# First two batches staged in the activation buffer of the feed-forward part, angle tables reduced on GpSimd, weights in gated chunks, second DFT product written densely

## The chip, the cores and the metric

One NeuronCore of a Trainium2 chip runs the whole program. The metric is the device time of one execution in microseconds (us); the times given are medians of timed runs. Engines are named as the profile names them: PE (matrix multiplication), ACT (scalar engine), DVE (vector engine), POOL (GpSimd), SP (the engine that issues most DMAs).

## The reference, cut to what matters

```python
q_n = q / (np.linalg.norm(q, axis=-1, keepdims=True) + 1e-06)      # q, k, v: (8, 12, 448, 64) f32
k_n = k / (np.linalg.norm(k, axis=-1, keepdims=True) + 1e-06)
scores = np.matmul(q_n, k_n.transpose(0, 1, 3, 2)) / tau           # tau = 0.1
attn = softmax(scores)
x = np.matmul(attn, v).transpose(0, 2, 1, 3).reshape(8, 448, 768)
mixed = np.real(np.fft.fft(np.fft.fft(x, axis=1), axis=2))
u = x + mixed
un = (u - mean(u)) / np.sqrt(var(u) + 1e-06)
out = u + np.maximum(un @ w_ch1, 0.0) @ w_ch2                      # w_ch1: (768, 3072), w_ch2: (3072, 768)
```

Every one of the eight batches goes through attention, a two-dimensional DFT, a layer norm and a feed-forward part. The weights are the same for all batches.

## The kernel before

All work is written as operations of a small planner (`Plan`): each has an engine (or two to choose from), an estimated duration, a priority and the names that it reads and writes. `schedule` simulates the engines with these estimates and fixes one order for each engine; `emit` writes the orders out with semaphore waits. At run time each engine takes its instructions strictly in that order, so one that has to wait holds up everything planned behind it.

Four stages are planned for each batch `b`:

- **Normalisation** (`attn`, first half). Seven tiles of 128 rows by 768 f32 are loaded (three of q, three of k, and one `t` with the last 64 rows of both), each as runs of 256 bytes, by SP into one of four staging slots `STG`. ACT squares a tile into `SQT` (L460), DVE sums it by head (L462), ACT takes Ln and Exp (L467, L470), DVE adds epsilon, takes the reciprocal (L472, L474) and scales the tile into a bf16 buffer `QH` (L480), and SP transposes it by DMA into `QT` or `KT` (L492). Four more loads bring v; POOL casts it into `VB` and `VZ`. POOL also copies one column of `QT` (`qdup`, L498), for which the score products wait.
- **Attention** for six pairs of heads: score products (L541 to L555), Exp on ACT (L532), products with v (L569, L572), and the division on DVE (L584, L586) into `X`. DVE then forms sums and differences `AC` (L594, L597).
- **DFT** (`fft`): DVE forms `F` from `AC` (L608), PE multiplies by the table over the sequence, `CSs` (24 matmuls, L622), ACT brings the result to SBUF (L633), PE multiplies by the table over the features, `CSd` (48 matmuls of 193 or 192 columns, L654), DVE adds `X` and writes `U` (L664, L666), and the layer norm writes `UN`, which SP transposes by DMA into `unT` (L704). There is one `UN` buffer, so each of three or four normalised tiles waits for the transposition ahead of it.
- **Feed-forward** (`ffn`): 24 groups `h` of six matmuls (L729) with Relu into `hT`, and then the products with `w_ch2` (L750), added to `U` (L759) and stored by SP or, through index lists, by POOL (L773). Batches with even `b` have three tiles of 128 rows, odd ones four.

Attention and DFT of a batch have the higher priority, the matmuls of the feed-forward part the lowest: they fill what is left of PE.

In L654 the output of a matmul goes to every second f32 word of a PSUM bank: `eo` is 0 for the even and 1 for the odd features, so that DVE can read the features in their natural order.

```python
lw = self.Tt[:, o0:o0 + 128]
m0, m1 = (0, 193) if eo == 0 else (193, 385)
...
r = pe.matmul(PS[:, bk + sg, eo:NL:2], lw, mv, start=(s == 0 and dj == 0),
```

The tables are made at the start: DVE forms the angles and reduces them by full turns (L370 to L384), and ACT takes the sines (L389 to L392); `hT`, which is not used yet, holds the temporary values. L393 then loads the table of functions that holds both Ln and Exp. The weights are cast to bf16 on the way by eight DMAs of 2.36 MB of f32 each, which POOL issues once all loads of batch 0 are issued (L405, L410).

## Time and profile before

| | us |
|---|---|
| median of 3 timed runs | 756.86 (756.28 to 757.26) |
| profiled execution, its own time | 761.87 |
| its span, first to last instruction | 760.1 |
| PE busy in the span | 642.2 |
| first matmul of the feed-forward part (L729) starts | 155.36 |

The profiled execution is 5.01 us longer than the median and 1.77 us longer than its span. Busy times of PE are modelled ends of pipelined matmuls; how fast a sequence of matmuls goes is read from the distance between starts.

### The profile page before, as it was taken

The page shows a single profiled execution, that of the slowest core. Times are in us where ns is not written, and L with a number is a line of the kernel's source. Part 1 is how long each engine was busy: PE and PEld are TensorE (multiplying, and loading weights), DVE is VectorE, ACT ScalarE, POOL GpSimd, SP SyncE. Part 2 cuts the span into 40 slices and gives each one's busy share as a digit, 9 for nine tenths or more (in the row PEclk, how much of TensorE's full clock was granted, in tenths as well). Part 3 has the DMA queues.
Part 4 walks back from the last instruction along what each step waited for, and adds up shares of the span by engine and source line. Part 5 has one row for each costly group of instructions (what it writes and reads, how often), then busy time and mean ns, then how long its engine had stood idle before and what let it go on. Part 6 is the DMA issues. An engine that isn't in the chain of part 4 may idle for free.

```text
span 760.1 us, 12228 instructions
## 1 busy us (share of the span) xinstructions
PE 642.2 (84%) x5088; PEld 392.4 (52%) x5088; DVE 343.7 (45%) x649; ACT 331.8 (44%) x561; POOL 62.7 (8%) x93
## 2 busy tenths in 40 slices
PE   0014146699999999999999999999999999999997
PEld 0002124467556556566655565567655756665454
DVE  8422144776665873865645546462244234000011
ACT  3333233764584784366426643463147320412400
POOL 3022001001002001010000010101010001001001
PEclk9999865999999999999999999999999999999999
DMA  4589999157749278526632474254111002101001
GB/s 83 112 159 199 202 194 199 36 98 165 146 89 189 47 129 165 131 54 146 136 87 44 71 139 104 61 108 63 33 42 22 1 22 63 43 22 42 0 22 63
DMA packets 206967, 70.79 MB, mean 93 GB/s; under 512 B 198464, under 2 KB 204608, under 8 KB 206912
## 3 DMA queue, kind: packets, MB, share of 16 engines
q1 hardware_dynamic: 199040, 52.71, 36.8%
q0 software_dynamic: 7872, 17.30, 9.7%
q8 instruction: 40, 0.66, 0.4%
q14 instruction: 15, 0.12, 0.1%
HBM read 51.90 MB, written 11.01 MB: 83 GB/s over the span
## 4 chain that ended last, share of the span: by engine, by line
PE 70%; DMA 13%; DVE 7%; ACT 5%; issue 3%; SPq 2%; POOL 0%; POOLq 0%; DVEq 0%; ACTq 0%
PE PS L729 27%; PE PS L750 23%; PE PS L654 8%; DMA STG<-in_k_dram 7%; PE PS L572 4%; DMA STG<-in_q_dram 3%; PE PS L541 3%; ACT E L532 2%; PE PS L622 2%; DVE QH L480 2%; DMA QT<-QH 1%; PE PS L545 1%; PE PS L569 1%; ACT SQT L460 1%; DVE SS L462 1%
## 5 line engine op out<-in xcount | busy, mean ns | idle before, releaser
L750 PE MATMUL PS<-W2b,hT 128*128 128x384 bf16 x1344 | 227.3, 326 | 0.0
L532 ACT ACTIVATE E<-PS 128x900 bf16<-128x900 f32 x192 | 150.7, 825 | 63.3 <-PE PS L545 56.2
L750 PEld LDWEIGHTS PS<-W2b,hT 128*128 128x128 bf16 x1344 | 129.1, 98 | 86.9 <-issue 5.0
L738 ACT ACTIVATE hT<-PS 128x384 bf16<-128x384 f32 (+1 forms) x153 | 83.0, 543 | 138.7 <-PE PS L729 138.2
L729 PE MATMUL PS<-unTo,W1b 128*128 128x512 bf16 x576 | 133.2, 380 | 0.5 <-DVE OUTB L759 0.5
L541 PE MATMUL PS<-QT,KT 64*128 64x225 bf16 x288 | 38.9, 277 | 85.5 <-POOL QT L498 52.5
L759 DVE TENSOR_TENSOR OUTB<-PS,U 128x384 f32<-128x384 f32 x56 | 31.1, 555 | 160.4 <-PE PS L750 160.3
L729 PE MATMUL PS<-unTe,W1b 128*128 128x384 bf16 x576 | 98.5, 326 | 1.7 <-DMA unTe<-UN 1.7
L462 DVE TENSOR_REDUCE SS<-SQT 128x12 f32<-128x768 f32 x56 | 52.9, 945 | 75.3 <-ACT SQT L460 75.1
L729 PEld LDWEIGHTS PS<-unTo,W1b 128*128 128x128 bf16 x576 | 54.2, 98 | 61.9 <-issue 3.2
L460 ACT ACTIVATE SQT<-STG 128x768 f32<-128x768 f32 x56 | 47.1, 841 | 87.8 <-DMA STG<-in_q_dram 38.7
L729 PEld LDWEIGHTS PS<-unTe,W1b 128*128 128x128 bf16 x576 | 55.4, 98 | 38.2 <-DMA unTe<-UN 2.0
L541 PEld LDWEIGHTS PS<-QT,KT 64*128 64x128 bf16 x288 | 14.2, 95 | 113.8 <-issue 63.0
L654 PE MATMUL PS<-CSd,AC 128*128 128x193 bf16 (+1 forms) x384 | 66.1, 374 | 3.7 <-ACT AC L633 2.9
L654 PEld LDWEIGHTS PS<-CSd,AC 128*128 128x128 bf16 x384 | 53.5, 140 | 15.5 <-ACT AC L633 3.9
L480 DVE TENSOR_TENSOR QH<-STG,RN 128x768 bf16<-128x768 f32 x56 | 55.0, 997 | 5.8 <-DMA KT<-QH 3.5
L572 PE MATMUL PS<-VB,E 128*128 128x65 bf16 x1152 | 55.6, 199 | 0.0
L569 PE MATMUL PS<-VZ,E 128*128 128x130 bf16 x192 | 44.0, 229 | 11.2 <-ACT E L532 9.1
L572 PEld LDWEIGHTS PS<-VB,E 128*128 128x128 bf16 x1152 | 52.2, 102 | 2.0
L773 POOL DMA_INDIRECT out_dram<-OUTB,IDX x20 | 19.6, 978 | 378.1 <-DVE OUTB L759 223.8
L502 POOL CAST VB<-STG 128x768 bf16<-128x768 f32 x24 | 20.4, 848 | 255.4 <-DMA STG<-in_v_dram 162.7
L666 DVE TENSOR_TENSOR U<-PS,X 128x385 bf16<-128x385 f32 (+3 forms) x40 | 22.4, 560 | 35.4 <-PE PS L654 34.7
(74 smaller groups left out, 444.2 us busy)
## 6 DMA issues: line engine op xcount, KB each, us to landing
STG<-in_q_dram SPq DMA_DIRECT2D x24, 384.0 KB, 5.1
STG<-in_k_dram SPq DMA_DIRECT2D x24, 384.0 KB, 5.5
STG<-in_v_dram SPq DMA_DIRECT2D x24, 384.0 KB, 5.3
W1b<-in_moe_w_ch_dram POOLq DMA_DIRECT2D x4, 1152.0 KB, 18.9
W2b<-in_moe_w_ch_dram POOLq DMA_DIRECT2D x4, 1152.0 KB, 43.3
out_dram<-OUTB SPq DMA_DIRECT2D x8, 384.0 KB, 2.3
STG<-in_q_dram SPq DMA_DIRECT2D x8, 192.0 KB, 3.4
STG<-in_k_dram SPq DMA_DIRECT2D x8, 192.0 KB, 4.5
```

The source lines that it names most:

```text
L460: P.add("act", lambda a, s=s: a.activation(self.SQT[:], self.STG[:, s, :], ACTF.Square), t_act(DM), pr, f"sq{i}_{b}", reads=[f"STG{s}"], w ...
L462: P.add("dve", lambda v, i=i: v.tensor_reduce(SS[:, i, :], v3(self.SQT[:]), AX.X, AluOp.add), t_dve(DM), pr, f"ss{i}_{b}", reads=["SQT"], ...
L480: P.add("dve", lambda v, i=i, s=s, r=r: v.tensor_tensor(v3(self.QH[:, r, :]), v3(self.STG[:, s, :]), RN[:, i, :].unsqueeze(2).to_broadcast ...
L532: return a.activation(o, self.PS[:, bk:bk + nc_, 0:SQ2], ACTF.Exp, scale=1.0 / self.tau)
L541: pe.matmul(self.PS[:, bk + h, 0:NK], self.KT[r, j, kt * 128:(kt + 1) * 128], self.QT[r, j, 0:NK], start=True, stop=True)
L569: pe.matmul(o, st(6), self.VZ[:, j, :], start=True, stop=False, skip_group_check=True)
L572: r = pe.matmul(o[:, 65 * h:65 * h + 65], st(2 * kt + h), self.VB[:, kt, 2 * j + h, :], start=False, stop=(h == 1 and kt == 2), skip_group ...
L654: r = pe.matmul(PS[:, bk + sg, eo:NL:2], lw, mv, start=(s == 0 and dj == 0), stop=(s == 1 and dj == 2))
L729: r = pe.matmul(self.PS[:, bk, 0:N], self.W1b[:, j, ft * 128:(ft + 1) * 128], unT[:, j, 0:N], start=(j == 0), stop=(j == NJ - 1))
L738: return e.activation(self.hT[:, ft, 0:N], self.PS[:, bk, 0:N], ACTF.Relu)
L750: r = pe.matmul(self.PS[:, bk, 0:384], self.hT[:, ft, 128 * i:128 * i + 128], self.W2b[:, ft, 384 * c:384 * c + 384], start=(ft == 0), sto ...
L759: return v.tensor_tensor(self.OUTB[:, ob, cs], self.PS[:, self.bank(tile), 0:384], self.U[:, ut, cs], AluOp.add)
```

## The change

- **Staging.** The q, k and `t` tiles of batches 0 and 1 go to `hT`, seven slots of three `hT` tiles each, instead of to the four slots of `STG`. All loads of batch 0 can so be issued at once; loads of v and of batch 1 are ordered behind chosen transpositions of batch 0 (`gates`), those of batch 2 behind the first store of an output. A Relu that writes an `hT` tile waits until batch 1 no longer needs that slot.
- **Squares.** For batch 0 they go to `E`, `SQT` and `OUTB`, so that they don't wait for each other's buffer. For batch 1 POOL multiplies the tile by itself, and all seven tiles form one group with one Ln, Exp and reciprocal. POOL may also scale tiles of batch 0.
- **Tables.** DVE only multiplies (five instead of ten products); POOL reduces 1605 values per row by full turns; cosines come from the sine with a bias of pi/2 and an added Abs on ACT. The sines, and the loading of the common table of Ln and Exp behind them, are planned after the last Exp of batch 0's normalisation.
- **Weights.** 24 chunks of 0.79 MB of f32 instead of eight of 2.36 MB. Each waits until the one two ahead of it has landed. The first chunk of `W1` waits for the last q/k load of batch 1, the first of `W2` for the last transposition of the normalised tiles of batch 0. The products wait for single chunks.
- **DFT product.** The second product writes 193 or 192 adjacent words; DVE reads even and odd features from the two halves with an access pattern.
- **Normalised tiles.** `UN` gets four buffers, which lie in `F`.
- **Planner.** DMAs get a latency and a service time on two shared queues; it knows orders without a wait.

```diff
+        dma_free = [0.0, 0.0]
...
+            if op.dma is not None:
+                i = 1 if e == "pool" and op.serve > 2 else 0
+                t0 = max(op.end + DMA_LAT, dma_free[i])
+                op.end = t0 + op.serve * (1.6 if dma_free[1 - i] > t0 else 1.0)
+                dma_free[i] = op.end
...
-        self.UN = T("UN", [128, DM])
-        self.unT = [T("unTe", [128, NJ, 384]), T("unTo", [128, NJ, 512])]
+        self.UN = self.F[:].rearrange("p a b c -> p (a b c)").rearrange("p (t c) -> p t c", t=4)
+        self.UNT = T("UNT", [128, NJ * 896])
+        self.unT = [self.UNT[:, 0:NJ * 384].rearrange("p (j c) -> p j c", j=NJ),
+                    self.UNT[:, NJ * 384:].rearrange("p (j c) -> p j c", j=NJ)]
...
+        P.add("pool", lambda g: [g.tensor_scalar(Qt[:, c], Pt[:, c], 1.0 / n, M, AluOp.mult, AluOp.add) for c, n in sect][-1],
+              1.9, -4, "tq", reads=["tp"], writes=["tq"])
+        P.add("pool", lambda g: [g.tensor_scalar(Qt[:, c], Qt[:, c], M, -float(n), AluOp.subtract, AluOp.mult)
+                                 for c, n in sect][-1], 1.9, -4, "tr", reads=["tq"], writes=["tq"])
+        P.add("pool", lambda g: g.tensor_tensor(Qt, Pt, Qt, AluOp.add), t_pool(nt, True), -4, "ts", reads=["tp", "tq"], writes=["tq"])
...
+            a.activation(self.CSs[:, :, 0, :], s2(Pt), ACTF.Sin, bias=h, scale=-w / S)
+            a.activation(self.CSs[:, :, 1, :], s2(Qt), ACTF.Sin, scale=w / S)
+            a.activation(self.CSd[:, :, 0, :], d3(Pt), ACTF.Sin, bias=h, scale=-w / DM)
+            a.activation(self.CSd[:, :, 1, :], d3(Qt), ACTF.Sin, scale=w / DM)
+            r = a.activation(self.CSd[:, :, 2, :], d3(Qt), ACTF.Sin, scale=-w / DM)
...
+    def tables(self):
+        P, sins = self.P, self.sins
+        Pt, Qt = self.temps
+        P.add("act", lambda a: a.activation(Pt, Qt, ACTF.Abs), t_act(3 * NL + 2 * NK), 9.5, "ta", reads=["tq"], writes=["tp"],
+              order=self.sq0)
+        P.add("act", sins, 1.3 + 4.3 + 1.3, 10.5, "sins", reads=["tp", "tq", "cst"], writes=["CSs", "CSd"], order=self.nrm0)
...
+    def weights(self, which, start):
         P = self.P
-        g0 = self.first_loads
-        for c in range(4):
-            P.add("pool", lambda g, s, c=c: g.dma_start(
-                self.W1b[:, :, c * 768:(c + 1) * 768],
-                self.w1.rearrange("(j p) f -> p j f", p=128)[:, :, c * 768:(c + 1) * 768]).then_inc(s, 16),
-                1.0, -3, f"w1_{c}", writes=[f"W1_{c}"], dma=(f"w1_{c}", 16), after=g0, lat=7.0 * (c + 1))
-        for c in range(4):
-            P.add("pool", lambda g, s, c=c: g.dma_start(
-                self.W2b[:, c * 6:(c + 1) * 6, :],
-                self.w2.rearrange("(t p) n -> p t n", p=128)[:, c * 6:(c + 1) * 6, :]).then_inc(s, 16),
-                1.0, -3, f"w2_{c}", writes=[f"W2_{c}"], dma=(f"w2_{c}", 16), after=g0, lat=7.0 * (c + 5))
+        prev = [start, start]
+        w1 = self.w1.rearrange("(j p) f -> p j f", p=128)
+        w2 = self.w2.rearrange("(t p) n -> p t n", p=128)
+        for i in range(12 * which, 12 * which + 12):
+            c = i % 12
+
+            def fn(g, s, i=i, c=c):
+                if i < 12:
+                    return g.dma_start(self.W1b[:, :, c * 256:(c + 1) * 256], w1[:, :, c * 256:(c + 1) * 256]).then_inc(s, 16)
+                return g.dma_start(self.W2b[:, c * 2:(c + 1) * 2, :], w2[:, c * 2:(c + 1) * 2, :]).then_inc(s, 16)
+            nm = f"W{1 + i // 12}_{c}"
+            prev.append(P.add("pool", fn, 1.0, 9, nm, writes=[nm], dma=(nm, 16), after=[prev[-2]], serve=2.1))
...
+            if b < 2 and kind != "v":
+                s = self.h_next % 7
+                self.h_next += 1
+                buf = self.hT[:, 3 * s:3 * s + 3, :].rearrange("p a b -> p (a b)").bitcast(F32)
+                names, key = [f"hT{3 * s + x}" for x in range(3)], f"lh{s}"
+            else:
+                s = self.stg_next % NSTG
+                self.stg_next += 1
+                buf, names, key = self.STG[:, s, :], [f"STG{s}"], f"ld{s}"
+
+            def fn(sy, sem):
+                for dst, src in dmas(buf):
                     sy.dma_start(dst, src).then_inc(sem, 16)
-            nd_ = len(dmas(self.STG[:, s, :]))
-            op = P.add("sp", fn, 0.36 * nd_, pr, f"ld_{nm}{b}", writes=[f"STG{s}"], dma=(f"ld{s}", 16 * nd_), lat=3.5)
+            nd_ = len(dmas(buf))
+            op = P.add("sp", fn, 0.36 * nd_, pr, f"ld_{nm}{b}", writes=names, dma=(key, 16 * nd_),
+                       order=[self.trs[gates[nm]]] if b < 2 and nm in gates else [self.first_st] if b == 2 else [],
+                       serve=0.8 if nm == "v3" else 1.6)
...
-        groups = [(0, 1), (2, 3), (4, 5), (6,)]
+        groups = [(0, 1), (2, 3), (4, 5), (6,)] if b != 1 else [tuple(range(7))]
+        if b == 0:
+            gates = dict(zip(("v0", "v1", "v2", "v3"), (1, 2, 3, 3)))
+        elif b == 1:
+            gates = {"q0": 4, "k0": 5, "q1": 6, "k1": 6, "q2": 6, "k2": 6, "t0": 6}
...
+                if b == 1:
+                    op = P.add("pool", lambda g, sq=sq, buf=buf: g.tensor_tensor(sq, buf, buf, AluOp.mult),
+                               t_pool(DM, True), pr, f"sq{i}_{b}", reads=names, writes=[sqn], margin=mg)
+                else:
+                    op = P.add("act", lambda a, sq=sq, buf=buf: a.activation(sq, buf, ACTF.Square),
+                      t_act(DM), pr, f"sq{i}_{b}", reads=names, writes=[sqn], margin=mg)
...
+                P.add(("dve", "pool") if b == 0 else ("dve",), lambda v, i=i, buf=buf, r=r: v.tensor_tensor(
+                    v3(self.QH[:, r, :]), v3(buf),
                     RN[:, i, :].unsqueeze(2).to_broadcast((128, H, DH)), AluOp.mult),
-                    t_dve(DM), pr, f"sc{i}_{b}", reads=[f"STG{s}", f"RN{par}_{i}"], writes=[f"QH{r}"])
+                    (t_dve(DM), t_pool(DM, True)), pr, f"sc{i}_{b}", reads=names + [f"RN{par}_{i}"], writes=[f"QH{r}"])
...
-                                r = pe.matmul(PS[:, bk + sg, eo:NL:2], lw, mv, start=(s == 0 and dj == 0),
+                                r = pe.matmul(PS[:, bk + sg, m0:m1], lw, mv, start=(s == 0 and dj == 0),
...
+                    src = PS[i0:i0 + n, bk, 0:NL]
+                    src = gp(src, [[-1, 192], [192, 2]], 192) if hi else gp(src, [[1, 192], [193, 2]])
+                    cs = slice(384, 768) if hi else slice(0, 384)
+                    return v.tensor_tensor(U[o0:o0 + n, ut, cs].rearrange("p (i e) -> p i e", e=2), src,
+                                           X[i0:i0 + n, x, cs].rearrange("p (i e) -> p i e", e=2), AluOp.add)
...
-            self.main = P.add("pe", fn, 6 * t_mm(N), PM, f"h{ft}_{b}", reads=un + [f"W1_{ft // 6}"], tiles=(tile,),
+            self.main = P.add("pe", fn, 6 * t_mm(N), PM, f"h{ft}_{b}", reads=un + [f"W1_{ft // 2}"], tiles=(tile,),
...
+                n = len(self.loads)
                 self.attn(b + 1)
+            if b == 0:
+                self.weights(0, self.loads[n + 6])
+                self.weights(1, self.last_tru)
```

The planner's new orders differ almost everywhere; three places of the start follow.

ACT in the normalisation of batch 0, **before**; SQT and E hold squares, SS sums of squares:

```order
L389 ACT_TABLE_LOAD
L389 ACTIVATE CSs<-F 128x900 [waits prog_dve]
L391 ACTIVATE CSd<-hT 128x3x770
L392 ACTIVATE CSd<-hT 128x3x385
L393 ACT_TABLE_LOAD
L467 ACTIVATE SS<-SS,cst 128x24 [waits prog_pool,prog_dve]
L460 ACTIVATE SQT<-STG 128x768 [waits prog_act,d_ld2]
L470 ACTIVATE SS<-SS 128x24 [waits prog_act]
```

The same place **in the changed kernel**, where L500 is the square, L511 Ln, L514 Exp:

```order
L500 ACTIVATE E<-hT 128x768 [waits d_lh2]
L511 ACT_TABLE_LOAD [waits prog_pool]
L511 ACTIVATE SS<-SS,cst 128x24 [waits prog_dve]
L500 ACTIVATE E<-hT 128x768 [waits d_lh3]
L514 ACT_TABLE_LOAD
L514 ACTIVATE SS<-SS 128x24 [waits prog_act]
L500 ACTIVATE SQT<-hT 128x768 [waits d_lh4]
L511 ACT_TABLE_LOAD
L511 ACTIVATE SS<-SS,cst 128x24 [waits prog_dve]
L514 ACT_TABLE_LOAD
```

The sines and the loading of the common table have moved behind the four groups of batch 0; in each group Ln and Exp now have a table load of their own, eight in all.

POOL at the weights, **before** (L502 and L506 cast v, L498 is the copy `qdup`):

```order
L498 COPY QT<-QT 128x6 [waits prog_dve,d_QT0,prog_pool,d_QT3,prog_act]
L502 CAST VB<-STG 128x12x64 [waits prog_pool,d_ld1]
L405 DMA W1b<-in_moe_w_ch_dram 128x6x768 [waits prog_pool,d_ld2]
L405 DMA W1b<-in_moe_w_ch_dram 128x6x768 x3
L410 DMA W2b<-in_moe_w_ch_dram 128x6x768 x4
L506 CAST VZ<-STG 64x6x64
```

POOL **in the changed kernel**, from the last squares of batch 1 (L497) to the `qdup` of batch 1 (L546); the left-out rows are five more chunks and the casts of v (L550, L554) between them:

```order
L423 DMA W1b<-in_moe_w_ch_dram 128x6x256 [waits prog_pool,d_lh6]
L423 DMA W1b<-in_moe_w_ch_dram 128x6x256
L497 TENSOR_TENSOR OUTB<-hT 128x768 [waits prog_dve,d_lh5]
L497 TENSOR_TENSOR SQT<-hT 128x768 [waits prog_pool,prog_dve]
L423 DMA W1b<-in_moe_w_ch_dram 128x6x256 [waits prog_pool,d_W1_0]
...
L423 DMA W1b<-in_moe_w_ch_dram 128x6x256 [waits d_W1_8]
L423 DMA W1b<-in_moe_w_ch_dram 128x6x256 [waits d_W1_9]
L424 DMA W2b<-in_moe_w_ch_dram 128x2x768 [waits d_unT0_2]
L424 DMA W2b<-in_moe_w_ch_dram 128x2x768
L546 COPY QT<-QT 128x6 [waits prog_act,d_QT3,d_QT0,prog_dve]
```

The weights now stand behind the loads of batch 1 instead of ahead of them, with waits in POOL's order, and `qdup` of batch 1 stands behind all chunks of `W1` and two of `W2`.

DVE ahead of batch 0's DFT, **before** (L594 to L608 make AC and F of batch 0; L462 to L480 normalise batch 1):

```order
L474 RECIPROCAL RN<-SS 128x24 [waits prog_dve]
L480 TENSOR_TENSOR QH<-STG,RN 128x768 [waits d_ld0,prog_dve,d_KT0]
L584 RECIPROCAL RD<-PS 128x8 [waits prog_pe]
L480 TENSOR_TENSOR QH<-STG,RN 128x768 [waits d_ld3,d_QT0]
L586 TENSOR_TENSOR X<-PS,RD 128x4x128 [waits prog_dve]
L462 TENSOR_REDUCE SS<-SQT 128x12 [waits prog_act]
L594 TENSOR_TENSOR AC<-X 128x2x384 [waits prog_dve]
```

and **in the changed kernel** (L504 sums, L518 adds epsilon for all seven tiles of batch 1, L633 to L647 make AC and F, L526 scales):

```order
L504 TENSOR_REDUCE SS<-OUTB 128x12 [waits prog_pool]
L504 TENSOR_REDUCE SS<-SQT 128x12 [waits prog_pool]
L623 RECIPROCAL RD<-PS 128x8 [waits prog_pe]
L625 TENSOR_TENSOR X<-PS,RD 128x4x128 [waits prog_dve]
L518 TENSOR_SCALAR SS<-SS 128x84 [waits prog_act]
L633 TENSOR_TENSOR AC<-X 128x2x384 [waits prog_dve]
L636 TENSOR_TENSOR AC<-X 128x2x384
L520 RECIPROCAL RN<-SS 128x84 [waits prog_dve]
L647 TENSOR_TENSOR F<-AC 128x1536 [waits prog_dve]
```

Before, scalings and loads of batch 1 through the four slots stood ahead of F; now the sums of all seven tiles of batch 1 do, and no scaling.

## Rows read from the trace of the kernel before

**Rows 1.** Two windows: length; busy PE, PEld, DVE, ACT, POOL; clock, DMA share, GB/s.

```profile
0.00:155.36 155.36, 49.24 (x506) 31.62 (x507) 69.45 (x123) 63.98 (x97) 21.95 (x43) 0.88 0.83 146
155.36:747.00 591.64, 585.33 (x4536) 356.42 (x4537) 272.65 (x524) 267.86 (x465) 38.83 (x48) 1.00 0.38 80
```

**Rows 2.** Chain that ended last, first 160 us: start us, us, what.

```profile
46.01 3.89 DMA QT<-QH
...
52.48 0.37 PE PS L541 x2
...
66.25 41.01 DMA STG<-in_k_dram
...
119.66 4.72 PE PS L622 x24
...
125.37 9.98 PE PS L654 x48
...
155.36 1.15 PE PS L729 x6
```

**Rows 3.** Timeline of PE at the end: start us, us, engine, line, operation.

```profile
645.43 23.56 PE L729 MATMUL PS<-unTe,W1b 128*128 128x384 bf16 x144
...
723.31 31.36 PE L750 MATMUL PS<-W2b,hT 128*128 128x384 bf16 x192
```

**Rows 4.** Chain, DFT products at the high clock: start us, us, what.

```profile
169.51 1.58 PE PS L622 x16
...
174.82 7.83 PE PS L654 x48
```

**Rows 5.** Groups on PE from 160 us on: busy us, mean ns, idle before.

```profile
L569 PE MATMUL PS<-VZ,E 128*128 128x130 bf16 x148 | 32.5, 220 | 1.1 <-ACT E L532 1.1
```

**Rows 6.** Window of the first 20 us; columns as in rows 1.

```profile
0.00:20.00 20.00, 0.00 (x0) 0.00 (x0) 15.21 (x22) 8.03 (x7) 7.08 (x23) 1.00 0.44 79
```

**Rows 7.** Timeline of the start, single instructions; columns as in rows 3.

```profile
0.75 0.46 SPq L431 DMA_DIRECT2D STG<-in_q_dram  x1
...
4.63 0.84 ACT L460 ACTIVATE SQT<-STG 128x768 f32<-128x768 f32 x1 [2.60 <-DMA STG<-in_q_dram]
...
20.27 1.28 ACT L393 ACT_TABLE_LOAD   x1
...
21.57 0.32 ACT L467 ACTIVATE SS<-SS,cst 128x24 f32<-128x24 f32 x1
...
32.45 1.27 SPq L492 DMA_TRANSPOSE KT<-QH  x1
...
53.08 3.02 ACT L532 ACTIVATE E<-PS 128x900 bf16<-128x900 f32 x4 [1.13 <-PE PS L545]
...
56.32 2.98 ACT L532 ACTIVATE E<-PS 128x900 bf16<-128x900 f32 x4 [0.22 <-PE PS L545]
```

**Rows 8.** Groups on POOL: busy us, mean ns, idle before.

```profile
L502 POOL CAST VB<-STG 128x768 bf16<-128x768 f32 x24 | 20.4, 848 | 255.4 <-DMA STG<-in_v_dram 162.7 <-PE PS L572 92.5
...
L405 POOL DMA_DIRECT2D W1b<-in_moe_w_ch_dram x4 | 3.6, 907 | 0.7 <-POOL VB L502 0.7
...
L397 POOL TENSOR_SCALAR CSs<-CSs 1x225 bf16<-1x225 bf16 x2 | 1.6, 792 | 11.9 <-ACT CSd L392 11.9
```

**Rows 9.** Timeline of SP, transpositions of batch 0's normalised tiles.

```profile
143.77 8.56 SPq L704 DMA_TRANSPOSE unTe<-UN  x3
```

**Rows 10.** Tile W1b: from issue to landing.

```profile
DMA to landing us min/median/max: 9.8/18.9/28.2
```

**Rows 11.** Tile W2b: from issue to landing.

```profile
DMA to landing us min/median/max: 34.3/43.3/52.3
```

**Rows 12.** Timeline of PE, two successive products with v, each one pair of 7 matmuls.

```profile
144.87 0.23 PE L569 MATMUL PS<-VZ,E 128*128 128x130 bf16 x1
...
145.12 0.22 PE L569 MATMUL PS<-VZ,E 128*128 128x130 bf16 x1
```

**Rows 13.** Costliest groups of the page: weight loads of the second product.

```profile
L654 PEld LDWEIGHTS PS<-CSd,AC 128*128 128x128 bf16 x384 | 53.5, 140 | 15.5 <-ACT AC L633 3.9
```

More of the change, by code (lines that the diff above doesn't have):

```diff
@@ L105, in add @@
         op.acquire = acquire
+        op.order = tuple(order)
         for t in tiles:
@@ L115, in schedule @@
         for op in self.ops:
-            cnt[op] = len(op.deps)
-            for d in op.deps:
+            cnt[op] = len(op.deps.union(op.order))
+            for d in op.deps.union(op.order):
                 nxt.setdefault(d, []).append(op)
@@ L124, in rtime @@
             for d in op.deps:
-                if d.eng == e and d not in op.raw:
+                if d.eng == e and d.dma is None and d not in op.raw:
                     t = max(t, d.start)
                 else:
-                    t = max(t, d.end + SEM_LAT)
-            return t + op.margin
+                    t = max(t, d.end + SEM_LAT + (op.margin if e == "pe" or d.dma is not None else 0.0))
+            return t
         def put(op):
@@ L394, in sins @@
             return r
-        P.add("act", sins, 1.3 + 4.0 + 1.3, 15, "sins", reads=["tp%d" % S, "tp%d" % DM] + wr, writes=["CSs", "CSd"])
+        self.sins, self.temps = sins, (Pt, Qt)
+    def tables(self):
[4 more added lines that the diff above has]
+        P.add("act", sins, 1.3 + 4.3 + 1.3, 10.5, "sins", reads=["tp", "tq", "cst"], writes=["CSs", "CSd"], order=self.nrm0)
@@ L469, in attn @@
                   0.25, pr, f"ln{b}", reads=ssn + ["cst"], writes=ssn)
-            P.add("act", lambda a, a0=a0, a1=a1: a.activation(SS[:, a0:a1, :], SS[:, a0:a1, :], ACTF.Exp, scale=0.5),
-                  0.2, pr, f"nrm{b}", reads=ssn, writes=ssn)
+            op = P.add("act", lambda a, a0=a0, a1=a1: a.activation(SS[:, a0:a1, :], SS[:, a0:a1, :], ACTF.Exp, scale=0.5),
+                       0.2, pr, f"nrm{b}", reads=ssn, writes=ssn)
+            if b == 0:
+                self.nrm0.append(op)
             P.add("dve", lambda v, a0=a0, a1=a1: v.tensor_scalar_add(SS[:, a0:a1, :], SS[:, a0:a1, :], 1e-6),
@@ L532, in fn @@
                     return a.activation(o, self.PS[:, bk:bk + nc_, 0:SQ2], ACTF.Exp, scale=1.0 / self.tau)
-                P.add("act", fn, t_act(nc_ * SQ2), pj, f"ex{j}_{b}", writes=nm, after=(tile.users[0],), tiles=(tile,))
+                P.add("act", fn, t_act(nc_ * SQ2), pj, f"ex{j}_{b}", writes=nm,
+                      after=[tile.users[0]] + (self.sqb if b == 0 and j < 2 else []), tiles=(tile,))
             for kt in range(3):
@@ L753, in ffn @@
                     self.main = P.add("pe", fn, 6 * t_mm(384), PM, f"y{i}{c}{q4}_{b}",
-                                      reads=[f"hT{ft}" for ft in range(6 * q4, 6 * q4 + 6)] + [f"W2_{q4}"],
+                                      reads=[f"hT{ft}" for ft in range(6 * q4, 6 * q4 + 6)] + [f"W2_{3 * q4 + x}" for x in range(3)],
                                       tiles=(tile,), acquire=(tile if q4 == 0 else None), after=[self.main])
```

161 lines of the change are left out of this document (74 added, 87 removed).

## Prediction

> **What bounds the kernel now.** I read the windows first, split where the feed-forward part starts. From 155.36 us on PE is busy for 585.33 of 591.64 us at the full granted clock, so 6.3 us are lost [rows 1]; every other engine has room. Ahead of that point PE is busy for 49.24 of 155.36 us, much of it at a lower clock. So the kernel is a slow start and then a long stretch of matmuls without gaps: only fewer us of matmul or an earlier start of the stretch count.
>
> The chain says why the start is slow. The first score product runs at 52.48 us; then one load of a k tile of batch 1 is on the chain for 41.01 us, from 66.25 on [rows 2]: it shares the DMA engines with the weights, all issued before. DVE, strictly in order, stands at that tile's sum, with the DFT of batch 0 behind it. The DFT follows at 119.66 and the feed-forward part at 155.36 [rows 2].
>
> The work of the long stretch, from starts of matmuls: two batches of the feed-forward part run from 645.43 to 723.31 + 31.36 = 754.67, so 109.2 us, and 437.0 for eight [rows 3]. The first DFT product takes 1.58/16 = 98.8 ns a matmul, 24 of them 2.37 us; the second takes 7.83 us for 48, 163 ns each [rows 4]; together 10.2. From 155.36 to 754.67 are 599.3 us, less 6.3 idle 593.0; less 437.0 and 7 x 10.2 = 71.4, attention has 84.6. The 148 products with VZ are 37 head pairs [rows 5], and about half a pair runs between 155.36 and 160: 2.26 us a pair. After the last matmul the span lasts 760.1 - 754.7 = 5.4 us.
>
> **The denser DFT product.** The first product writes 225 adjacent words in 98.8 ns, the second 193 words at stride two in 163 ns [rows 4]; both change weights for each matmul. No row shows 193 adjacent words. Bounds: 163 ns (the stride is not the cause) and 98.8 x 193/225 = 84.7 ns. I take the lower, from the row of the same kind of matmul: 48 x 84.7 = 4.07 us, 3.76 less for each DFT, 26.3 for the seven in the long stretch. DVE reads as many words as before, in another pattern; unknown between nothing and twice its time, covered by PE's other work except in the first DFT, where it could add 4 us.
>
> The Trainium skill, "TensorE: Matmul & The Clock Gate", section "LDWEIGHTS", speaks against that much: 128 columns of weights would take some 107 ns, and by it the product would stay at 5.1 us, some 7.5 us less gain in all. This trace disagrees: seven matmuls, each with its own weights, start every 145.12 - 144.87 = 0.25 us, 36 ns apart [rows 12].
>
> **The start in the changed kernel**, step by step, up to the first feed-forward matmul (T):
> - Loads. Four loads in the first 20 us keep the DMA engines busy for 0.44 x 20 = 8.8 us, 2.2 us each [rows 6]. The first, issued at 0.75, is squared at 4.63 [rows 7]: 1.7 us beside its 2.2. The third lands at 9.0, the seventh at 17.8.
> - ACT from 9.0 on has no pause: five squares of 0.84, Abs over 1605 values (1.75 at the rate of a square), eight table loads of 1.28 (this is new: before, the common table came first), four Ln and four Exp of at most 0.32 [rows 7]: 18.8, so 27.8. Two more table loads and the sines of 4365 values, 4.8 us by that rate, keep it to 35.
> - The last tile: 1.4 us on DVE, then a transposition of 3.89 [rows 2] ends at 33, hidden under the sines. Before, 2.6 us lay between landing (49.90) and the first score product (52.48); of these 1.1 remain after 35: 36, against 52.48.
> - Attention of batch 0 at ACT's pace, 56.32 - 53.08 = 3.24 us a pair [rows 7]: 19.4, and 1 to 2 for the last product: 57.
> - Batch 1. SP issues v and then batch 1 behind the last transposition (27.8 + 1.4 + 1.27 [rows 7]), from 30.5 on: 9.5 tiles of 2.2 and 1.7, so the last q/k tile lands at 53. POOL then issues two chunks (0.9 each) and does two squares. The trace has no f32 product on POOL: bounds are a cast of 768 values, 0.85, and a tensor-scalar at 0.79 for 225, 2.7 for 768 [rows 8]. A product reads two inputs where the cast reads one, so I take twice the cast, 1.7: 53 + 1.8 + 3.4 = 58.2. A sum, Ln, Exp and epsilon add 1.8, AC and half of F 2: the DFT of batch 0 starts at 62. It is this wait, not attention's end, that comes last.
> - The DFT. Before, first product to second took 125.37 - 119.66 = 5.7, with 4.72/24 = 197 ns a matmul: twice the 98.8 of later, so the lower clock level [rows 2, 4]. PE comes from a pause again, so I take 5.7, and 2 x 4.07 = 8.1 for the second: 75.8.
> - From there to the feed-forward part: 155.36 - 125.37 - 9.98 = 20.0 before [rows 2]. In that, three transpositions through one buffer took 8.56 us to issue [rows 9]; with four buffers three issues of 1.27 follow each other, 3.8: 15.3. T = 91. Against this stands `qdup`, which waits behind POOL's chunks; see the weights.
>
> Bounds of T: 80 (DFT at the high clock, 6.9 less; squares as fast as a cast, 1.7 less; loads at 2.0 us, 2 less) and 104 (squares at 2.7 on seven tiles that then trail the loads, 4; 20.0 instead of 15.3; slow DVE reads, 4).
>
> **The weights.** Between the landings of the first and the last of four DMAs are 52.3 - 34.3 = 18.0 us [rows 11]: 6.0 each, 2.0 for one third. The first of all took 9.8 [rows 10], 3.8 beside its 6.0. With two in flight a chunk costs (0.9 + 3.8 + 2.0)/2 = 3.35 us; the lower bound is 2.0. W1 then lands until 53 + 12 x 3.35 = 93, W2 at 93 + 40 = 133. `qdup` comes at about 93, when PE has other groups `h`. PE needs the last quarter of W2 after T + 23.4 (24 groups) + 13.6 (attention of batch 1) + 6.4 (its DFT) + 3 of the first output tile, and some 8 of waits: 145. So 12 us to spare, and I cost the chunks at nothing; beyond 4 us a chunk the cover is gone. POOL's 16 more issues lie in its idle time.
>
> The Trainium skill, "DMA: Bandwidth & Descriptors", section "Bandwidth", speaks against the small chunks: it asks for 1 MiB or more per DMA, and its fit (2.0 us plus bytes) would give 3.8 us for one of 0.79 MB, nearly the point where the cover ends if nothing overlapped. No row shows a DMA of this size.
>
> **Sum.** From T on: 437.0 + 42 x 2.26 + 7 x 6.44 = 577.0 of matmuls. Waits: 6.3 before; attention of batch 1 now runs inside the first feed-forward part, at ACT's pace and partly at the lower clock, so I take 12 (6 to 20). 91 + 577.0 + 12 + 5.4 = 685.4, 74.7 less than the span of 760.1. The profiled execution itself took 761.87, the median 756.86; the difference taken off the median gives **682 us**. With the bounds of T and of the waits: 665 to 702, and 668 to 700 as this case's own range.
>
> **Rivals.**
> - *Weights late*: chunks cost 4.5 to 6 us, because a chunk's fixed time isn't hidden. W2 lands at 53 + 24 x 5 = 173 for 5 us, 28 after PE needs it: **710**. For it: waits of POOL in its own order, transposes and v loads among the chunks. Against: 9.8 us for a DMA three times as large, under load [rows 10]. The page on DMA names such a cost.
> - *The product stays as it was*, the stride not being the cause: 682 + 26.3 and 1.9 in the first DFT: **710**. For it: no row of adjacent 193. Against: the dense 225 [rows 4].
> - *Weight loads bound the product*: 48 of 140 ns [rows 13] are 6.7 us instead of 4.07, 2.65 x 7 more: **701**. Against: rows 12. The page on TensorE names weight loads as such a cost.
> - *Slower*: the chunk chain starves PE. The gain of 75 is used up when W2 lands at 145 + 75 = 220, that is at (220 - 53)/24 = 7 us a chunk; at 8 it is 245, and **782**. Against: it needs twice the 3.35.
>
> **Chances.** Forecast 0.65, weights late 0.17, product as before 0.07, weight loads 0.06, slower 0.04, and 0.01 for a chunk right at 7 us, which ends within 0.2%, about what a measurement of this kernel can tell from no change. So faster 0.95, same 0.01, slower 0.04. The range 666 to 714 leaves out the slower case, the late half of the late weights and the edge of the forecast, under 2 in 10.
>
> **What would show it.** L693 at 4.1 us for 48 matmuls at the full clock (not 7.8); eight table loads ahead of the sines; first score product at 36; the last square of batch 1 on POOL ahead of the first matmul of the DFT, at 62; first L770 at 91; chunks of weights every 3.4 us, and no wait of PE's L791 for a DMA. The forecast is wrong if L693 keeps 163 ns, if POOL's squares take over 3 us, or if PE waits for W1b, W2b or `qdup` for more than 10 us.

## The result, and the profile after

The changed kernel takes **684.86 us** (median of four runs, 679.65 to 685.53) against 757.06 for the kernel before on the same chip: ratio 0.903, with a 95% interval of 0.899 to 0.908. The forecast was 682, the range 666 to 714. It is near, but partly by luck: the start was 6 us longer than forecast, the waits behind it 10 us shorter, and 5 us were taken off at the end without a reason.

The windows of the changed kernel, split at the first feed-forward matmul, columns as in [rows 1]:

```profile
0.00:97.35 97.35, 27.43 (x324) 18.82 (x325) 55.25 (x88) 51.94 (x69) 48.98 (x61) 0.84 1.10 162
97.35:676.73 579.38, 577.50 (x4764) 350.49 (x4764) 280.02 (x541) 284.05 (x490) 48.40 (x62) 1.00 0.48 94
```

The long stretch starts 58 us earlier than in [rows 1] and has 1.9 us of idle PE where 6.3 were. It ends with the last products:

```profile
645.37 31.36 PE L791 MATMUL PS<-W2b,hT 128*128 128x384 bf16 x192
```

The second DFT product, by the page's costliest groups and by the timeline of batch 1's DFT: 4.01 us from its start to the start of what follows, 83.5 ns a matmul, where [rows 4] had 163. (The 253 ns of the group's row are the length of one record; the records of successive matmuls overlap.) DVE's sums that read the new layout take 550 ns each, no more than before (560).

```profile
L693 PE MATMUL PS<-CSd,AC 128*128 128x193 bf16 (+1 forms) x384 | 35.1, 253 | 1.6 <-ACT AC L672 1.6
...
L706 DVE TENSOR_TENSOR U<-PS,X 128x384 bf16<-128x384 f32 (+3 forms) x80 | 40.6, 550 | 35.1 <-PE PS L693 34.0
```

```profile
141.75 4.18 PE L693 MATMUL PS<-CSd,AC 128*128 128x193 bf16 x48
145.76 1.46 PE L791 MATMUL PS<-W2b,hT 128*128 128x384 bf16 x8
```

The start is shown by a timeline of single instructions. There are table loads between ACT's Ln and Exp, the first score product comes at 34.19 ([rows 2]: 52.48), and then comes the place that the forecast missed. The last sum of squares (L504) is done at 57.9, but ACT stands for 6.65 us at a copy of half of batch 1's v tail (L824), the last 64 rows of v, which have not landed yet, and Ln (L511) is behind it:

```profile
4.67 0.84 ACT L500 ACTIVATE E<-hT 128x768 f32<-128x768 f32 x1 [2.66 <-DMA hT<-in_q_dram]
9.14 1.28 ACT L511 ACT_TABLE_LOAD   x1
...
24.60 1.28 ACT L514 ACT_TABLE_LOAD   x1
25.89 0.21 ACT L514 ACTIVATE SS<-SS 128x12 f32<-128x12 f32 x1
...
34.19 0.37 PE L580 MATMUL PS<-QT,KT 64*128 64x225 bf16 x2 [34.19 <-POOL QT L546]
...
55.42 1.47 POOL L497 TENSOR_TENSOR SQT<-hT 128x768 f32<-128x768 f32 x1
56.92 0.95 DVE L504 TENSOR_REDUCE SS<-SQT 128x12 f32<-128x768 f32 x1 [0.59 <-POOL SQT L497]
...
61.62 0.53 ACT L824 ACTIVATE VZ<-STG 64x384 bf16<-64x384 f32 x1 [6.65 <-DMA STG<-in_v_dram]
62.18 0.36 ACT L511 ACTIVATE SS<-SS,cst 128x84 f32<-128x84 f32 x1
...
66.46 4.70 PE L661 MATMUL PS<-CSs,F 128*128 128x225 bf16 x24 [10.23 <-DVE F L647]
72.18 5.86 PE L693 MATMUL PS<-CSd,AC 128*128 128x193 bf16 x48 [1.01 <-ACT AC L672]
97.35 7.80 PE L770 MATMUL PS<-UNT,W1b 128*128 128x384 bf16 x30 [19.31 <-DMA UNT<-F]
```

From the DFT's end (78.04) to the feed-forward part are 19.3 us. The end of this stretch, on the chain: the last normalised tile is ready at 87.6, but SP (L745) is then still issuing the transposition of the second tile, until 91.42. The last one is issued at 91.47 and lands 5.84 us later. Beside it POOL issues weight chunks until 92.49.

```profile
87.10 0.47 DVE F L741
87.58 0.88 DVE QH L526
88.45 2.96 SPq L745
91.42 0.05 issue
91.47 5.84 DMA UNT<-F
```

SP's timeline has the three tiles (L745) and a transposition of batch 1 between them. The second of the three takes 3.51 us to issue, the first 1.21; they land 8.1, 8.7 and 5.8 us after the start of their issue:

```profile
84.48 1.21 SPq L745 DMA_TRANSPOSE UNT<-F  x1
85.88 1.97 SPq L538 DMA_TRANSPOSE QT<-QH  x1
87.91 4.98 SPq L745 DMA_TRANSPOSE UNT<-F  x2
```

### The profile page after: what moved, and what is told of

It is laid out like the page before. It is cut to its first block, busy times and chain, and to the rows that moved or that the text cites. A ratio compares the mean times of both kernels' runs of the same rounds, so it can differ in the third digit from the quotient of the medians.

```text
span 682.8 us, 12274 instructions
## 1 busy us (share of the span) xinstructions
PE 604.9 (89%) x5088; PEld 369.3 (54%) x5088; DVE 335.8 (49%) x630; ACT 336.0 (49%) x559; POOL 98.3 (14%) x124
## 4 chain that ended last, share of the span: by engine, by line
PE 81%; DMA 6%; ACT 5%; DVE 3%; SPq 2%; issue 2%; POOL 0%; POOLq 0%; DVEq 0%; ACTq 0%
PE PS L770 33%; PE PS L791 29%; PE PS L693 4%; PE PS L611 4%; PE PS L580 3%; PE PS L661 3%; DMA hT<-in_q_dram 2%; PE PS L584 2%; PE PS L608 2%; SPq L452 1%; DMA STG<-in_v_dram 1%; ACT E L570 1%; DMA STG<-in_q_dram 1%; DMA UNT<-F 1%; DMA QT<-QH 1%
## 5 line engine op out<-in xcount | busy, mean ns | idle before, releaser
L770 PE MATMUL PS<-UNT,W1b 128*128 128x512 bf16 (+1 forms) x1152 | 233.7, 356 | 19.3 <-DMA UNT<-F 19.3
L770 PEld LDWEIGHTS PS<-UNT,W1b 128*128 128x128 bf16 x1152 | 110.1, 98 | 119.4 <-DMA UNT<-F 19.5
L580 PE MATMUL PS<-QT,KT 64*128 64x225 bf16 x288 | 37.3, 269 | 39.1 <-POOL QT L546 34.6
L706 DVE TENSOR_TENSOR U<-PS,X 128x384 bf16<-128x384 f32 (+3 forms) x80 | 40.6, 550 | 35.1 <-PE PS L693 34.0
L780 DVE TENSOR_SCALAR hT<-PS 128x512 bf16<-128x512 f32 (+1 forms) x45 | 28.3, 628 | 43.9 <-PE PS L770 43.6
L504 DVE TENSOR_REDUCE SS<-SQT 128x12 f32<-128x768 f32 x46 | 43.3, 942 | 11.6 <-ACT SQT L500 10.7
L500 ACT ACTIVATE SQT<-STG 128x768 f32<-128x768 f32 x42 | 35.4, 842 | 20.2 <-DMA STG<-in_q_dram 8.4
L608 PE MATMUL PS<-VZ,E 128*128 128x130 bf16 x192 | 42.5, 222 | 1.1 <-ACT E L570 1.1
L550 POOL CAST VB<-STG 128x768 bf16<-128x768 f32 x24 | 22.0, 916 | 135.6 <-DMA STG<-in_v_dram 81.0
L736 ACT ACTIVATE RS<-MV,cst 128x1 f32<-128x1 f32 x28 | 8.1, 293 | 67.7 <-DVE MV L734 67.6
L526 DVE TENSOR_TENSOR QH<-STG,RN 128x768 bf16<-128x768 f32 x42 | 39.9, 968 | 0.8
L693 PE MATMUL PS<-CSd,AC 128*128 128x193 bf16 (+1 forms) x384 | 35.1, 253 | 1.6 <-ACT AC L672 1.6
L584 PE MATMUL PS<-QT,KT 64*128 64x225 bf16 x288 | 36.4, 263 | 0.0
```

The source lines that it names most:

```text
L504: op = P.add("dve", lambda v, i=i, sq=sq: v.tensor_reduce(SS[:, i, :], v3(sq), AX.X, AluOp.add), t_dve(DM), pr, f"ss{i}_{b}", reads=[sqn], ...
L526: P.add(("dve", "pool") if b == 0 else ("dve",), lambda v, i=i, buf=buf, r=r: v.tensor_tensor(v3(self.QH[:, r, :]), v3(buf), RN[:, i, :].u ...
L580: pe.matmul(self.PS[:, bk + h, 0:NK], self.KT[r, j, kt * 128:(kt + 1) * 128], self.QT[r, j, 0:NK], start=True, stop=True)
L584: i = pe.matmul(self.PS[:, bk + h, NK:SQ2], self.KT[r, j, kt * 128:(kt + 1) * 128], self.QT[r, j, S:NK - 2:-1], start=True, stop=True)
L608: pe.matmul(o, st(6), self.VZ[:, j, :], start=True, stop=False, skip_group_check=True)
L693: r = pe.matmul(PS[:, bk + sg, m0:m1], lw, mv, start=(s == 0 and dj == 0), stop=(s == 1 and dj == 2))
```

## The experiments

"T" is the first feed-forward matmul, "DFT" the first product of batch 0's DFT, both in the profiled run. The kernel before was timed anew beside each group of kernels (757 to 763 us), so ratios are compared, not times. Unless said otherwise an experiment starts from the changed kernel and leaves every other engine's order as it is. Of the five lowest ratios, neighbours have overlapping intervals: which of two neighbours is the faster is not shown.

| kernel | us | ratio to before (interval) | DFT | T |
|---|---|---|---|---|
| changed | 684.86 | 0.903 (0.899 to 0.908) | 66.46 | 97.35 |
| strided product again | 710.57 | 0.937 (0.933 to 0.940) | 67.28 | 98.44 |
| before + dense product alone | 742.56 | 0.979 (0.977 to 0.981) | 119.97 | 151.70 |
| v tail's copy later | 678.47 | 0.893 (0.890 to 0.895) | 62.03 | 90.31 |
| common table first | 681.14 | 0.897 (0.896 to 0.898) | 64.87 | 92.95 |
| both of these | 676.44 | 0.890 (0.887 to 0.892) | 62.74 | 91.07 |
| table operations on DVE | 685.19 | 0.900 (0.898 to 0.903) | 70.03 | 99.80 |
| all three | 673.49 | 0.887 (0.884 to 0.889) | 60.41 | 88.81 |
| all three, normalised tiles first | 674.59 | 0.888 (0.885 to 0.891) | 61.37 | 87.13 |
| weights early, ungated | 718.78 | 0.947 (0.944 to 0.950) | 105.91 | 128.56 |
| the same, v tail's copy later | 716.39 | 0.941 (0.936 to 0.945) | 80.22 | 129.09 |
| weights in large DMAs | 680.28 | 0.894 (0.891 to 0.898) | 66.48 | 89.64 |
| what gained, together | 674.57 | 0.885 (0.882 to 0.888) | 57.78 | 84.71 |

**The product at stride two again.**

```diff
-  r = pe.matmul(PS[:, bk + sg, m0:m1], lw, mv, ...
+  r = pe.matmul(PS[:, bk + sg, eo:NL:2], lw, mv, ...
```

> The changed kernel with the second DFT product writing every second word again, and the sums that read it as before; all else as changed, every engine's order too. My theory (the stride alone makes the 163 ns): 48 matmuls cost 7.8 us instead of 4.0 in the seven later DFTs, 26.8 us more, and 2 to 4 more in the first: 714 us, 711 to 718. Rival (the matmuls are only part, and waits for weight loads or for DVE's sums end the DFT anyway): at most a third of it shows, 694 us or less.

The sums on DVE read the old layout again here. Measured: 0.034 of 757 is 25.6 us more, a little under what my theory had, with T 1.1 later. The page gives the product's 384 matmuls 63.9 us of busy time instead of 35.1, so the stride is what makes the 163 ns. The first DFT's product did lose 2.1 us (8.00 instead of 5.86), but T moved by only half of that.

```profile
L693 PE MATMUL PS<-CSd,AC 128*128 128x193 bf16 (+1 forms) x384 | 63.9, 367 | 1.8 <-ACT AC L672 1.8
```

**The dense product alone, in the kernel before.** The same edit the other way, and the sums' pattern with it.

> The kernel before with nothing changed but the dense write of the second DFT product and the sums that read it. My theory (the two halves of the change add up): 26.8 us less in the seven later DFTs and 2 to 4 in the first, so 727 us, 724 to 730. Rival (the stretch of matmuls isn't so full that a shorter DFT counts; DVE's sums or ACT come last there): 735 to 745 us.

Measured: 16.7 us less, the rival's range. T fell by 3.7. From T to the last matmul's end it went from 599.3 [rows 2, 3] to 584.2, 15.1 less; seven products that take 4.01 instead of 7.83 us are worth 26.7, so 11.6 were lost again. PE is idle for 17.5 us of that stretch, where it was for 6.3. The longest of PE's waits after T (engine, line, released by: us, times, longest):

```profile
PE PS L730 <- ACT hT L739: 4.9, 2, 3.3
PE PS L654 <- ACT E L532: 3.0, 1, 3.0
PE PS L541 <- DVE U L667: 2.4, 2, 2.0
```

In the longest of them ACT, in order, stands at the square of a late load, with the next group's Relu (L739) behind it:

```profile
182.02 0.84 ACT L460 ACTIVATE SQT<-STG 128x768 f32<-128x768 f32 x1 [3.40 <-DMA STG<-in_q_dram]
182.77 0.85 ACT L739 ACTIVATE hT<-PS 128x384 bf16<-128x384 f32 x2
```

So the two halves of the change don't add up: 16.7 alone, 25.6 in the changed plan.

**The v tail's copy behind Ln and Exp of batch 1.** `nrm1` is that Exp.

```diff
-  self.copy(self.VZ[64:128, ...], vw[64:128], ..., margin=mg)
+  self.copy(self.VZ[64:128, ...], vw[64:128], ..., margin=mg,
+            order=[self.nrm1] if b == 1 else [])
```

> The changed kernel with ACT's copy of batch 1's v tail moved behind batch 1's Ln and Exp; every other engine's order is unchanged. My theory (ACT stood for the v tail until 61.62 while the sums were ready at 57.9): Ln at about 58, the DFT of batch 0 starts at 62.5 instead of 66.46, the feed-forward part at 93 to 94 instead of 97.35, and the time falls by about 4 us, to 681. Rival (transpositions of the normalised tiles, slow beside the weight chunks, end last whatever comes before): the DFT starts earlier, but the feed-forward part still starts at 96 to 98, and the time stays within 1 us of 684.9.

Measured, in the timeline: Ln at 58.04, the copy still at 61.60, the DFT at 62.03, the forecast's 62. T came 7.0 earlier, more than the 4.4 at the DFT. Of the rest, 1.7 are the second product, which ran at a granted clock of 1.00 (2.4 GHz) in 4.19 us, where it had 0.70, partly 1.2 GHz, and 5.86 us; no run shows why the clock rose sooner.

```profile
58.04 0.36 ACT L511 ACTIVATE SS<-SS,cst 128x84 f32<-128x84 f32 x1 [1.91 <-DVE SS L504]
...
61.60 0.53 ACT L826 ACTIVATE VZ<-STG 64x384 bf16<-64x384 f32 x1 [2.89 <-DMA STG<-in_v_dram]
```

**The common table first, both, and the table operations on DVE.** The first is one preload of the table ahead of the first square; the third moves the five operations on 1605 values (`tq`, `tr`, `ts`) from POOL to DVE, behind `prods`.

```diff
+  pre = b == 0 and i == 0
...
+      if pre:
+          self.nc.scalar.preload_act_table_set("natural_log_exp_and_others")
+      return a.activation(sq, buf, ACTF.Square)
...
+  tb = [op for op in po if op.name in ("tq", "tr", "ts")]      # po, do: the orders of POOL and DVE
+  i = [op.name for op in do].index("prods") + 1
+  for op in tb:
+      po.remove(op)
+      op.eng = "dve"
+  do[i:i] = tb
```

> The changed kernel with ACT's common table (with Ln, Exp and Square) loaded once ahead of the first square, so that eight table loads of 1.28 us go; nothing else moves. My theory (ACT is the pace of the start): ACT still waits for the tables' POOL part, done at 17.4, before Abs; so the last Exp ends at about 20 instead of 26.1, the first score product comes at 28 instead of 34.2, batch 1's loads and the feed-forward part 6 us earlier (91), and the time falls by 6 us, to 679. Rival (loads or POOL's work set the pace of batch 1, not ACT): the first score product comes earlier, but the feed-forward part at 96 to 98, and the time stays within 1 us of 684.9.

> The changed kernel with the five table operations (remainder of the products) given back to DVE, behind its products; nothing else moves. My theory (POOL's table work and DVE's two-input work hold each other up, and ACT's eight table loads set the pace of the start anyway): the first pair of scalings takes about 1.9 us instead of 5.16, the first score product stays at 34 to 35, the time within 1.5 us of 684.9. Rival (DVE, now with 5 us more ahead of the first sums, becomes the pace): the first score product at 37 or later, and 687 us or more.

> The changed kernel with both single changes, the v tail's copy behind batch 1's Ln and Exp and the common table loaded first. My theory (they remove two different waits, so what each gained adds up, less what the tables' change had already taken from the v tail's wait): the DFT of batch 0 starts at 60 instead of 66.46, the feed-forward part at 86 to 88.5, 674 to 676 us. Rival (the weights are then too late: the last chunk of W2 lands at about 131 whatever comes before, and PE needs it some 50 us after the feed-forward part starts): PE waits for W2b, and the time stays at 678 us.

> Both single changes and the five table operations on DVE, together. My theory (with the table loads gone, the start hangs on DVE, and there on the time in which POOL's table work holds it up: a scalar operation of 0.2 took 3.5 us beside it): the last transposition of batch 0 is issued 2 to 3 us earlier than the 27.7 us seen with the table change alone, the feed-forward part starts at 84 to 86.5, and the time is 672 to 674 us. Rival (DVE's own 5 us of table work take the place of the hold-up): no earlier than with both changes, 674 to 677 us.

Measured: the table alone brings the first score product from 34.19 to 31.64, not to 28, and 0.6% of the time. What then holds the start is DVE beside POOL. With the table change, a scalar operation on 24 values takes 3.54 us and ends only when POOL's sum of 1605 does (timeline of that kernel):

```profile
7.50 5.98 POOL L385 TENSOR_SCALAR UNT<-UNT 128x1155 f32<-128x1155 f32 x2
...
13.80 4.15 POOL L387 TENSOR_TENSOR UNT<-U,UNT 128x1605 f32<-128x1605 f32 x1
...
14.44 3.54 DVE L524 TENSOR_SCALAR SS<-SS 128x24 f32<-128x24 f32 x1
```

In the changed kernel two of DVE's scalings take 5.16 us beside the same sum. The first of them ends only behind it: from the sum's end at 17.36 to the scalings' end at 19.04 are 1.7 us, about what the pair takes alone. POOL's second pair of table operations (L385) takes 5.98 us, the like pair before it 1.81. That is not DVE's doing: it takes 5.98 to 6.01 in all eight of these kernels that leave it on POOL, also with the table first, where DVE's work beside it lies at other times. Why it is so slow there stays open.

```profile
5.38 1.81 POOL L383 TENSOR_SCALAR UNT<-U 128x1155 f32<-128x1155 f32 x2 [0.19 <-POOL VZ L362]
...
7.49 5.98 POOL L385 TENSOR_SCALAR UNT<-UNT 128x1155 f32<-128x1155 f32 x2
...
13.79 3.57 POOL L387 TENSOR_TENSOR UNT<-U,UNT 128x1605 f32<-128x1605 f32 x1
13.88 5.16 DVE L526 TENSOR_TENSOR QH<-hT,RN 128x768 bf16<-128x768 f32 x2
```

With the same operations on DVE, each pair takes 1.07 and the scalings 1.83:

```profile
5.02 1.07 DVE L383 TENSOR_SCALAR UNT<-U 128x1155 f32<-128x1155 f32 x2
6.13 1.06 DVE L385 TENSOR_SCALAR UNT<-UNT 128x1155 f32<-128x1155 f32 x2
...
15.32 1.83 DVE L526 TENSOR_TENSOR QH<-hT,RN 128x768 bf16<-128x768 f32 x2
```

Alone that gains nothing, as my theory had it, though the first score product comes at 35.92, a little after the 34 to 35 expected; with the table loads gone it brings that product to 28.94. "Both" missed its 86 to 88.5 for T: Ln came at 57.24, but DVE, beside POOL's casts of v, took 1.25 and 1.17 us for sums that last 0.55 otherwise, so the DFT was no earlier than with the copy alone, and the ratio is not clear of that run's. Its rival, W2 late, did not happen: PE waited for no W2b. "All three" met its time, though not its T: 88.8 for 84 to 86.5, and its ratio is not clear of that of "both".

**Normalised tiles first.** Batch 1's last three scalings (DVE) and transpositions (SP) behind batch 0's three tiles.

> Both single changes and the tables on DVE, and on DVE and SP batch 1's last three scalings and transpositions behind batch 0's three normalised tiles instead of between them. My theory (of the 19 us from the DFT's end to the feed-forward part, SP's order and the crowd of transpositions on the DMA engines make some 5): the third tile's transposition is issued at 79 instead of 82.3, it lands in 4 to 6 us instead of 8.5 since fewer are in flight, the feed-forward part starts at 84 to 86 instead of 88.8, and the time is 669 to 671 us. Rival (the weight chunks alone make the landing slow, or the score products of batch 1 then come late and PE waits for them): 672.5 us or more.

Measured: the rival's time. The third tile's transposition was issued at 79.74 instead of 82.31, about as expected, but it landed 7.14 us later, where "all three" had 6.46. T was 1.7 earlier, and the ratio is within the interval of "all three". SP's order is worth 1.7 us at T; it is not what makes the landing slow. The chain:

```profile
79.74 7.14 DMA UNT<-F
```

**The weights early and ungated.** The plan is made as in the changed kernel; then POOL's 24 chunk issues move to the old place and lose their waits on each other.

```diff
   self.est = self.P.schedule()
+  for op in ws:                      # ws: POOL's 24 chunk issues
+      po.remove(op)
+      op.deps = set(self.loads[:11])
+  i = [op.name for op in po].index("vz_0")
+  po[i:i] = ws
```

> The changed kernel with all 24 weight chunks issued ungated at the place in POOL's order that the weights had before, behind batch 0's loads; every other engine's order is unchanged. My theory (the late, gated weights are what lets batch 1 load early; seven buffers alone don't): batch 1's loads share the DMA engines with 18.9 MB of weights again, its last k tile lands near 100 instead of 53, the feed-forward part starts at 130 to 150 instead of 97.35, and the time is 715 to 735 us. Rival (the seven buffers in the feed-forward activations are what matters, since the loads are queued ahead of the weights' bulk): within 10 us of 684.9.

> The weight chunks early and ungated, as in the run before (718.8 us), and ACT's copy of batch 1's v tail behind batch 1's Ln and Exp. My theory, corrected by that run (the seven buffers let batch 1's q and k tiles through by 70; it was the v tail, landed at 102, with ACT's copy ahead of Ln, that held the DFT of batch 0 until 105.9): Ln at 74, the DFT of batch 0 at 78 to 80, the feed-forward part at 100 to 106, 686 to 692 us. Rival (my first theory: the loads as such are too late under the ungated weights): the DFT after 95, and 705 us or more.

Measured: the time of my first theory, by another mechanism. Batch 1's last q/k tile is squared at 70.59, 15 us later than in the changed kernel, and POOL's issues alone, 38.09 to 56.7, are enough for that; the tiles were not late by 50. What held the DFT until 105.91 was again the v tail, with Ln at 102.61:

```profile
102.05 0.53 ACT L824 ACTIVATE VZ<-STG 64x384 bf16<-64x384 f32 x1 [26.98 <-DMA STG<-in_v_dram]
```

The second kernel has the copy behind Ln and fell short of its 686 to 692, since the copy is still ahead of the three copies (L674) between the DFT's products. ACT's timeline there:

```profile
76.50 0.36 ACT L511 ACTIVATE SS<-SS,cst 128x84 f32<-128x84 f32 x1 [1.02 <-DVE SS L504]
...
105.97 0.53 ACT L826 ACTIVATE VZ<-STG 64x384 bf16<-64x384 f32 x1 [28.80 <-DMA STG<-in_v_dram]
106.52 1.73 ACT L674 ACTIVATE AC<-PS 128x900 bf16<-128x900 f32 x2
```

The first product did start at 80.22, about as expected; the wait moved two instructions on. So the late, gated weights are worth 33 us here, and in both of these traces it is v, queued behind q and k, on which ACT waits. What a kernel would take in which nothing of the DFT waits for v was not tried.

**The weights in four and four DMAs**, gated two ahead as the chunks were.

> The changed kernel with the weights in four and four DMAs, three chunks in one, still two in flight and at the same places in POOL's order; all else unchanged. My theory (PE waits for no weights in the changed kernel, and the pace is that of the DMA engines, not a fixed cost of a chunk): within 3 us of 684.9, W1 landed at about the same time as with chunks. Rival (a small DMA carries a fixed cost that large ones save): W1 landed by 86 instead of some 100, the transpositions beside it shorter, the feed-forward part at 92 to 94 and 679 to 681 us. Second rival (two DMAs three times as large crowd out the v tail and the transpositions): the feed-forward part after 101, 689 us or more.

Measured: the first rival. POOL's timeline: the fourth and last DMA of W1 is issued at 68.34 and, at 13.8 us at most from issue to landing, is in by 82.2. With chunks the twelfth is issued only at 92.49.

```profile
51.09 1.09 POOL L862 DMA_DIRECT2D W1b<-in_moe_w_ch_dram  x1 [3.60 <-DMA hT<-in_k_dram]
...
68.34 0.82 POOL L862 DMA_DIRECT2D W1b<-in_moe_w_ch_dram  x1 [3.88 <-DMA W1b<-in_moe_w_ch_dram]
89.67 0.82 POOL L864 DMA_DIRECT2D W2b<-in_moe_w_ch_dram  x1 [20.51 <-DMA UNT<-F]
```

So no weights are in flight when the normalised tiles are transposed: the last takes 2.82 us instead of 5.84 on the chain, and from the DFT's end to T are 13.5 us. That is 5.8 of the 7.7 us by which T is earlier; 1.7 more are the second product, at the full clock again (4.19). With the weights early, where they have landed by then too, the stretch to T is 13.3 us, so in these runs the weight traffic is what makes it long. The chain's line:

```profile
86.57 2.82 DMA UNT<-F
```

The queue of the weights between 60 and 98 us (packets, MB, time that the packets took as a share of 16 engines), first with chunks, then with large DMAs: 501 bytes a packet against 1504, and less of the engines' time for more bytes.

```profile
q0 software_dynamic: 7604, 3.81, 83.3%
```

```profile
q0 software_dynamic: 3172, 4.77, 72.7%
```

The length of the packets is not all of it. W2's chunks have packets nearly as long as the large DMAs (1446 and 1501 bytes), and no transpositions beside them; still they moved 3.14 MB in the 22 us from 108 on, the large ones 3.18 MB in the 16 us from 97 on. The run changes the size of a DMA and the amount in flight together; small chunks with more of them in flight were not tried.

**What gained, together.** The table first, its operations on DVE, the large DMAs, and the v tail's copy behind the DFT's three copies.

> What the runs showed to gain, in one kernel: the common table loaded first, the table operations on DVE, the weights in four and four gated DMAs, and ACT's copy of batch 1's v tail behind the three copies of batch 0's DFT (in the run with the weights early it held these copies up). My theory (the start's waits are separate, and large DMAs leave the transpositions of batch 0's normalised tiles free, 13.5 us from the DFT's end to the feed-forward part instead of 19): the DFT starts at 60.5, its second product ends at 70, the feed-forward part starts at 83 to 84.5, and the time is 667 to 669.5 us. Rival (with an earlier start the large DMAs still run beside the transpositions, or W2 comes late): the feed-forward part at 87 or later, or a wait of PE for W2b, and 672 us or more.

Measured: DFT 57.78, T 84.71, just past the expected 84.5, and no wait for W2b; but 674.57 us, beside 762.60 for the kernel before, is the rival's time. By ratio, 0.885, it is the lowest, yet inside the interval of "all three" (0.887). The DFT's end to T was 17.3 again: an earlier DFT meets the last two large DMAs of W1 once more.

## Why the prediction was right, and where not

- **Dense product**: right. 83.5 ns for 84.7 predicted, and the strided write costs 25.6 us. By the Trainium skill, "TensorE: Matmul & The Clock Gate", section "LDWEIGHTS", a weight load of 128 columns would take some 107 ns (an estimate from its formula); the trace shows 83.5 ns a matmul with new weights each time, so the loads don't bound the product. DVE's other reading pattern cost nothing.
- **Start up to attention's end**: right within 2 us. The first loads land every 1.8 us, not 2.2; the last Exp ends at 26.1 (27.8), eight table loads of 1.28 included; the first score product comes at 34.19 (36), attention's last product ends at 56.2 (57). POOL's square takes 1.47 (1.7).
- **"It is this wait, not attention's end, that comes last"**: the step that failed. The last squares were summed at 57.9, but the DFT started at 66.46, not 62, because ACT stood at the v tail's copy with Ln behind it. Without that copy ahead of Ln it starts at 62.03. That this is the computed 62 is in part luck: the squares end 1.2 us sooner than computed, and from there the DFT is 1.2 us further, 0.6 of it a reciprocal (L520) that the sum left out. The prediction read ACT's own work and not what else the plan put into ACT's order between Exp and Ln. The section on the kernel before has POOL casting v; the second half of its tail goes to ACT or DVE, as the planner chooses, and for batch 1 that was ACT.
- **5.7 and 8.1 for the DFT**: 5.72, and 5.86 for the second product, 2.2 less than predicted: the granted clock was 0.50 until it began, as assumed, but 0.70 during it.
- **15.3 from the DFT to T**: 19.3. The three issues were taken at 1.27 each, one behind the other, and the landing as before. Beside the weight chunks the second took 3.51 to issue, behind a transposition of batch 1, and the last landed after 5.84, where it was 4.20 before. With the weights landed the stretch is 13.5. Together with the two points before (4.5 late, 2.2 saved) this makes T 97.35 for 91.
- **Weights at nothing**: right for PE, which waited for none, wrong for the transpositions. The chunks of W1 were issued every 3.7 us, those of W2 every 2.9 (3.35 predicted). The rule on DMA size that the prediction cited (the Trainium skill, "DMA: Bandwidth & Descriptors", section "Bandwidth", 1 MiB or more for each) agrees with the run in which three chunks made one DMA of 2.36 MB: T came 7.7 us earlier, 5.8 of them behind the DFT. The cost of small chunks came by another way than that of the "weights late" rival.
- **577.0 of matmuls from T on**: 577.5. **Waits of 12**: 1.9, a term over-sized by 10. From T on the changed plan waits less than the old one (6.3), though batch 1's attention moved in. Which part of the new plan does it was not tried by itself; the dense product in the old plan waits more, not less.
- **Span to time**: 97.35 + 579.38 + 6.1 = 682.8 for 685.4. The 5.0 us between the profiled execution before and its median were carried over, and shouldn't have been: the profiled execution after took 684.6, its median is 684.86. Late start, short waits and this step nearly cancel, which is why 682 came so near.
